# Sixteen of 32 re-laid v reads issued on ScalarE instead of SyncE, with the instruction order searched anew, in a fused attention and GEGLU block

## The chip, the cores and the metric

One core of one Trainium2 chip runs the whole program. The metric is device time in microseconds (us), the median of several executions. The kernel before takes 245.5 us; the span inside its profiled execution, first to last instruction, is 243.3 us. Executions of one kernel on one chip mostly agree within 0.3%.

## The reference, cut to what matters

```python
h = layernorm(x) * (1 + ca) + sa              # x: 2048 tokens x 512
qkv = h @ wqkv                                # 32 heads of 16
# each token looks at itself and 7 earlier tokens, 2 apart (W, dil = 8, 2)
logits = einsum('bhsd,bhswd->bhsw', q, kg) * scale ; attn = softmax(logits)
o = einsum('bhsw,bhswd->bhsd', attn, vg)
x = x + ga * (o @ wo)
h = layernorm(x) * (1 + cb) + sb
x = x + gb * ((gelu(h @ w_gate) * (h @ w_up)) @ w_down)     # 1792 wide
```

## The kernel before: the parts concerned

The tokens go through in five groups (256, 256, 512, 512, 512), called group 0 to group 4. VectorE multiplies q with shifted k (tiles `pq`) and the weights `e` with shifted v (tiles `pv`); TensorE adds the products up by matmuls. For the second product v must lie in another layout, `vR`: four blocks of 32 partitions, each shifted by two tokens more. The kernel writes v to a scratch buffer in DRAM (`scr`) and reads it back four times, about 260 KB each. That makes 8 x 4 = 32 reads, all on SyncE:

```python
for r in (0, 2, 1, 3):
    dma(P * njv * (n + 8) * 2, lambda dq, ...: dq.dma_start(
        out=t[32*r:32*r + 32, ...], in_=bass.AP(scr..., offset + 2 + 2*r, ...)),
        r=[scr], w=[(t, r)], ..., bw=185e3, late=0.7)
```

The program is a list of 1016 operations. `ORDER`, a constant list of their numbers found by a search on a planning model, fixes in which order they are emitted, and so the order on every engine.

```python
placed = [self.ops[i] for i in ORDER]
...
for o in placed:
    ...                 # take buffers, warm-up matmuls before the first real one
    o.fn()
```

The DMA semaphores are eight and go round over both queues: a transfer waits until the one eight places earlier in the list has landed.

## Time and profile before

| | before |
|---|---|
| time, median | 245.5 us |
| span of the profiled run | 243.3 us |
| first real matmul (`qkv_ps`) | 12.14 us |
| end of the last matmul | 239.41 us |
| **stream** (the difference) | **227.27 us** |
| tail after it | 3.87 us |

The last three rows are read from the timeline of PE. The span is the start plus the stream plus the tail. A stream consists of matmuls at their cadence (0.216 us for one of 512 columns in this trace) and of holes, in which TensorE stands. The prediction shows the other lines of this profile.

### The profile page before, as it was taken

Reading aid. Unit: us, or ns where it says so; the run is one execution under the profiler, and the core shown is the slowest. Engines: PE = TensorE matmul, PEld = TensorE weight load, DVE = VectorE, ACT = ScalarE, POOL = GpSimd, SP = SyncE. Lnnn points to the kernel's source line nnn. Section 1 sums busy time; section 2 is a strip of 40 time slices with the busy share of each in tenths; the row PEclk is TensorE's granted clock in tenths of the full one; section 3 lists DMA queues with packets and bytes.
Section 4 is the critical chain, followed back from the end, with each engine's and each line's share of the span. In section 5 each row is a group of like instructions: output and inputs, shape, how many; then the busy total and the mean of one; then the engine's idle time right before and its main releaser. Section 6 shows DMA issues by size and latency. Waiting matters only on the chain.

```text
span 243.3 us, 4304 instructions
## 1 busy us (share of the span) xinstructions
PE 235.3 (97%) x1660; PEld 128.2 (53%) x1680; DVE 163.4 (67%) x317; ACT 148.5 (61%) x278; POOL 25.7 (11%) x45
## 2 busy tenths in 40 slices
PE   7999999999999999999999999999999999999993
PEld 2499555644469645775443444444444444444461
DVE  3878998999999999669985577982422413221222
ACT  2288799678958763894588865328467442665400
POOL 1287212002000300120000011000000100000000
PEclk9999999999999999999999999999999999999999
DMA  5999999898999338269022904210000412000011
GB/s 162 354 316 270 195 195 211 201 238 197 270 285 274 110 94 178 60 180 142 11 65 57 221 9 90 43 43 1 3 0 0 108 26 86 0 0 0 3 43 43
DMA packets 38970, 29.10 MB, mean 120 GB/s; under 512 B 14117, under 2 KB 38054, under 8 KB 38950
## 3 DMA queue, kind: packets, MB, share of 16 engines
q1 hardware_dynamic: 38800, 28.83, 49.8%
q8 instruction: 13, 0.21, 0.4%
q14 instruction: 7, 0.06, 0.1%
q10 hardware_dynamic: 150, 0.00, 0.0%
HBM read 21.40 MB, written 4.28 MB: 106 GB/s over the span
## 4 chain that ended last, share of the span: by engine, by line
PE 70%; DVE 17%; DMA 5%; issue 2%; POOL 2%; ACT 2%; DVEq 0%; ACTq 0%; POOLq 0%
PE y_ps L827 20%; PE u_ps L800 20%; PE g_ps L800 19%; PE x_ps L777 4%; DVE pq L654 4%; DMA wqkv<-in_A_wqkv_dram 3%; DVE pq L660 3%; DVE pv L752 3%; PE o_ps L762 2%; POOL rstd L522 2%; DVE st L516 2%; PE LT L670 2%; PE qkv_ps L603 1%; DVE xn L526 1%; DMA x_sg<-in_A_x_dram 1%
## 5 line engine op out<-in xcount | busy, mean ns | idle before, releaser
L800 PE MATMUL u_ps<-h2T,Wu 128*128 128x512 bf16 (+1 forms) x280 | 54.4, 336 | 0.5 <-ACT gl L809 0.3
L800 PE MATMUL g_ps<-h2T,Wg 128*128 128x512 bf16 (+1 forms) x280 | 54.7, 337 | 0.1
L827 PE MATMUL y_ps<-WdP,hht 128*128 128x512 bf16 (+1 forms) x230 | 49.1, 366 | 0.4
L809 ACT ACTIVATE gl<-g_ps 128x512 bf16<-128x512 f32 x56 | 33.0, 603 | 25.1 <-PE g_ps L800 24.8
L603 PE MATMUL qkv_ps<-hT,wqkv 128*128 128x512 bf16 (+1 forms) x229 | 43.7, 339 | 0.1
L812 DVE TENSOR_TENSOR hht<-gl,ub 128x512 bf16<-128x512 bf16 x56 | 22.6, 422 | 28.8 <-ACT ub L811 20.3
L811 ACT CAST ub<-u_ps 128x512 bf16<-128x512 f32 x56 | 31.7, 589 | 14.9 <-PE u_ps L800 11.7
L800 PEld LDWEIGHTS <-Wg 128*128 128x128 bf16 x280 | 27.0, 98 | 23.0 <-issue 1.5
L800 PEld LDWEIGHTS <-Wu 128*128 128x128 bf16 x280 | 27.0, 98 | 22.7 <-issue 2.0
L827 PEld LDWEIGHTS <-hht 128*128 128x128 bf16 x238 | 23.1, 98 | 24.6 <-issue 0.4
L522 POOL TENSOR_TENSOR rstd<-rstd,neghalf 128x2 f32<-128x2 f32 x16 | 17.5, 1094 | 162.4 <-DVE rstd L511 140.1
L603 PEld LDWEIGHTS <-wqkv 128*128 128x128 bf16 x232 | 24.9, 114 | 13.6 <-issue 1.3
L654 DVE TENSOR_TENSOR pq<-qT,kT 128x2048 bf16<-128x2048 bf16 x24 | 28.8, 1215 | 0.3
L746 DVE TENSOR_TENSOR pv<-e,vR 128x2048 bf16<-128x2048 bf16 x24 | 28.5, 1219 | 0.0
L538 ACT ACTIVATE h2T<-h2T,modT,scl 128x512 bf16<-128x512 bf16 (+1 forms) x20 | 13.2, 726 | 15.1 <-DMA h2T<-xn 15.1
L840 DVE TENSOR_TENSOR ot<-y_ps,x_sg 128x512 bf16<-128x512 f32 (+1 forms) x13 | 8.2, 648 | 18.5 <-PE y_ps L827 18.5
L781 DVE SCALAR_TENSOR_TENSOR x_sg<-x_ps,x_sg 128x512 bf16<-128x512 f32 x16 | 11.0, 687 | 14.2 <-PE x_ps L777 7.2
L777 PE MATMUL x_ps<-woP,oT 128*128 128x512 bf16 x57 | 14.9, 379 | 0.7 <-DVE rinv L723 0.5
L508 ACT ACTIVATE xn<-x_sg,xsum 128x512 bf16<-128x512 bf16 x16 | 11.5, 721 | 4.3 <-DVE xsum L505 4.3
L516 DVE BATCH_NORM_STATS2 st<-x_sg 128x6 f32<-128x512 bf16 x16 | 10.6, 679 | 3.3 <-DMA x_sg<-in_A_x_dram 3.3
L619 ACT CAST kT<-qkv_ps 128x512 bf16<-128x512 f32 x16 | 9.5, 602 | 1.8 <-PE qkv_ps L603 1.8
L619 ACT CAST qT<-qkv_ps 128x512 bf16<-128x512 f32 x16 | 9.5, 600 | 1.3 <-PE qkv_ps L603 1.3
(93 smaller groups left out, 201.2 us busy)
## 6 DMA issues: line engine op xcount, KB each, us to landing
vR<-scr SPq DMA_DIRECT2D x24, 260.0 KB, 5.0
wm<-in_w_mod_dram SPq DMA_DIRECT2D x6, 512.0 KB, 6.7
vR<-scr SPq DMA_DIRECT2D x8, 264.0 KB, 5.2
out_dram<-ot SPq DMA_DIRECT2D x15, 128.0 KB, 1.8
Wg<-in_B_w_gate_dram SPq DMA_DIRECT2D x2, 896.0 KB, 11.0
Wu<-in_B_w_up_dram SPq DMA_DIRECT2D x2, 896.0 KB, 5.4
WdP<-in_B_w_down_dram SPq DMA_DIRECT2D x2, 896.0 KB, 12.6
scr<-vT SPq DMA_DIRECT2D x6, 264.0 KB, 2.4
```

What stands on the lines that cost most here:

```text
L516: dve(0.59, lambda i=i, st=st, c0=c0: nc.vector.bn_stats(out=st[:, i, :], in_=x[g, c0 + i]), r=[x.key(g, c0 + i)], w=[(st, i)], pri=p)
L522: gp(0.65, lambda rstd=rstd: nc.gpsimd.tensor_tensor(out=rstd[:], in0=rstd[:], in1=neghalf[:, 0:2], op=ALU.pow), r=[rstd, neghalf], w=[rst ...
L603: nc.tensor.matmul(ps[:, j - j0, :], lhsT=wqkv[b][:, dt, j:D:4], rhs=h_cols(hT, g, dt), start=(dt == 0), stop=(dt == DT - 1))
L619: act(0.475, lambda t=t, off=off, j0=j0, ps=ps: nc.scalar.copy(out=t[:, j0:j0 + nj, off:off + n], in_=ps[:]), r=[ps], w=[(t, j) for j in r ...
L654: dve(1.14, lambda j=j, wg=wg, t=pq[m]: nc.vector.tensor_tensor(out=t[:], in0=_ap(q[g][:, j, 0:n], [[0, 4], [1, n]]), in1=_ap(k[g][:, j, : ...
L746: dve(1.14, lambda jj=jj, jl=jl, wg=wg, t=pv[m]: nc.vector.tensor_tensor(out=t[:], in0=_ap(e[:, wg, :], [[0, 4], [1, n]]), in1=vR[g][jj][: ...
L777: nc.tensor.matmul(x1_ps[:], lhsT=oT[:, j, c4 * P:(c4 + 1) * P], rhs=woP[:, j, :], start=(j == 0), stop=(j == 3))
L800: nc.tensor.matmul(ps[:, ft - f0, :], lhsT=Wt[ft // 7][:, dt, ft % 7 * P:(ft % 7 + 1) * P], rhs=h_cols(h2, g, dt), start=(dt == 0), stop=( ...
L809: act(0.485, lambda gl=gl, ps=gu[0]: nc.scalar.activation(out=gl[:], in_=ps[:], func=ACT.Gelu_apprx_tanh), r=[gu[0]], w=[gl], pri=p, table ...
L811: act(0.475, lambda ub=ub, ps=gu[1]: nc.scalar.copy(out=ub[:], in_=ps[:]), r=[gu[1]], w=[ub], pri=p)
L812: dve(0.335, lambda gl=gl, ub=ub, ht=ht: nc.vector.tensor_tensor(out=ht[:], in0=gl[:], in1=ub[:], op=ALU.mult), r=[gl, ub], w=[ht], pri=p)
L827: nc.tensor.matmul(y_ps[:], lhsT=hh[ft // nf][:, ft % nf, c4 * P:(c4 + 1) * P], rhs=WdP[:, ft, c0:c0 + w], start=(ft == 0), stop=(ft == FT ...
```

## The change

The intent: half of the issues leave SyncE, on which a blocked read holds up what follows, and the order is searched again. The diff, cut:

```diff
 ORDER = [
-    55, 5, 0, 7, 8, 9, 42, 43, 40, 41, 2, 6, 13, 33, ...
+    56, 7, 0, 55, 1, 4, 8, 9, 40, 42, 41, 33, 5, 6, ...
     (all 1016 numbers anew)
...
-        lat = {... "pool": 0.45 ...}
+        lat = {... "pool": 0.15 ...}
...
-                    r=[scr], w=[(t, r)], ..., bw=185e3, late=0.7)
+                    r=[scr], w=[(t, r)], ..., bw=300e3, late=0.7,
+                    ring="act" if r > 1 else "sp")
```

`lat`, `bw`, the planner's one shared pipe and some durations (cut here) are only the planner's picture of the chip; on the chip they show through the order alone, and in one warm-up matmul more (14 for 13). One more planner's rule is cut here: the matmuls of the last output tile's two halves may only come after those of the other tiles (`after=ends`). This rule asks for a half tile at the very end.

## The prediction

> **What bounds the kernel now.** I began with the share of busy time and the chain that ended last.
>
> ```profile
> PE 235.3 (97%) x1660; PEld 128.2 (53%) x1680; DVE 163.4 (67%) x317; ACT 148.5 (61%) x278; POOL 25.7 (11%) x45
> PE 70%; DVE 17%; DMA 5%; issue 2%; POOL 2%; ACT 2%; DVEq 0%; ACTq 0%; POOLq 0%
> ```
>
> The first line says that TensorE is busy for 97% of 243.3 us, the second that 70% of the chain is matmuls and 17% VectorE. A busy PE can still be a slow one, so next I cut the span into stages (columns: stretch, its length, then the busy time of PE, weight loads, DVE, ACT and POOL with counts, granted clock, DMA share, GB/s):
>
> ```profile
> 0.00:12.00 12.00, 10.29 (x75) 4.64 (x76) 7.70 (x24) 2.39 (x6) 2.86 (x13) 1.00 0.82 257
> 12.00:66.00 54.00, 52.77 (x509) 33.94 (x513) 50.21 (x96) 45.13 (x86) 15.62 (x25) 1.00 1.03 232
> 66.00:160.00 94.00, 93.18 (x683) 52.93 (x690) 80.20 (x141) 63.06 (x117) 5.84 (x5) 1.00 0.53 123
> 160.00:220.00 60.00, 59.74 (x296) 26.73 (x300) 19.80 (x46) 32.33 (x62) 1.42 (x2) 1.00 0.09 23
> 220.00:243.30 23.30, 19.31 (x102) 9.97 (x102) 5.45 (x12) 5.53 (x11) 0.00 (x0) 1.00 0.07 23
> ```
>
> In the first 12 us PE only runs warm-up matmuls until the first third of wqkv lands; that wait stands in the chain as a DMA piece. From 12 to 220 us PE is busy for 52.77 + 93.18 + 59.74 = 205.69 of 208 us, so **all idle time there is 2.3 us**. The PE timeline shows the real matmuls starting at 12.14 us and ending at 239.42 us, and inside that stretch 16 matmuls of 128x512 take 3.46 us, 0.216 us each, with a granted clock of 1.00 throughout. PE is packed with work that has to be done. After it 3.9 us are left: one last addition on VectorE (0.69 us), the issue of the last store and its landing, and the program's end.
>
> Where the 2.3 us go, from the waits of PE:
>
> ```profile
> PE x_ps L777 <- DVE rinv L723: 0.5, 1, 0.5
> PE LT L700 <- DVE m L695: 0.4, 1, 0.4
> PE u_ps L800 <- ACT gl L809: 0.3, 1, 0.3
> ```
>
> Two are waits for VectorE, in the stage from 12 to 66 us, where VectorE is busy 93% of the time (50.21 of 54); that is also where the chain runs over VectorE. None is for a v read.
>
> Last I asked after the tile vR, the re-laid v, which this change is about, and after what the queue on SyncE waits for:
>
> ```profile
> L628 SPq DMA_DIRECT2D vR<-scr x32: 538/594/1010, 26.3 to 148.3; - x32
> L746 DVE TENSOR_TENSOR pv<-e,vR x24: 1212/1220/1225, 77.7 to 164.5; 128x2048 bf16<-128x2048 bf16 x24
> L752 DVE TENSOR_TENSOR pv<-e,vR x8: 1218/1220/1226, 38.5 to 61.1; 128x2048 bf16<-128x2048 bf16 x8
> DMA to landing us min/median/max: 3.6/5.1/10.9
> ...
> SPq L628 <- DVE pv L746: 8.1, 2, 6.3
> ```
>
> 32 reads, 0.594 us of issue each, 5.1 us to land; and the tile's list of what ended idle time before the products pv is empty: **no product of the kernel before waits for its v**. The last line says that it is the other way round in one place: SyncE's queue stood 6.3 us at one read until a product had freed the buffer, with everything behind it in that queue.
>
> **What the Trainium skill says.** "DMA: Bandwidth & Descriptors", section "Issuing engines are not separate DMA queues": transfers of all issuing engines run on the same 16 DMA engines, and using several issuers saves only the issuing sequencer's time. Not shown before, because but for four tiny loads all transfers go on SyncE; it means that I count no bandwidth as won. The same page, "Queues, rings and completion order", says that SP and ACT each own a row of rings and that an engine takes turns between the rows it has work for, packet by packet. So a read on ScalarE's ring need not wait behind megabytes queued on SyncE's. The trace before shows such queueing: the two reads issued at 49.7 and 50.3 us, behind a 0.9 MB load of Wg, took 10.6 and 10.7 us to land instead of 5.1. "Perfetto Trace Analysis", "Sequencer Loop": a sequencer reads one instruction after the other, so a transfer that must wait holds what follows on its engine; the 6.3 us above agree.
>
> **The change part by part.** I numbered the program's 1016 operations in the order in which it makes them, which the change keeps, and read both order lists by engine.
>
> 1. *SyncE loses 16 issues*: 16 x 0.594 = 9.5 us of its sequencer. It is idle for most of the span (77.2 us in waits for the norm's output alone), so nothing of it is on the path. Worth 0 directly.
> 2. *ScalarE gains 16 issues*: 16 x 0.594 = 9.5 us, on top of 148.5 us. From 12 to 66 us it is busy 45.1 of 54; I count four of the reads before its first gelu instruction's stage and some four near 66 us: up to 8 x 0.594 = 4.8 us, which makes 49.9 of 54. The new order also moves three evacuations of group 4's q and k (0.48 us of cadence each, 1.4 us) behind the first gelu, against one before. It still fits, with little slack. Later (66 to 160 us) ScalarE has 31 us free. On the path: 0 as long as no issue has to wait; PE has four one-bank buffers ahead of ScalarE, about 3.5 us of work, to ride over 0.6 us.
> 3. *Reads land earlier*, by the queueing they escape, up to some 5 us for those behind weights. Since no product waits for them now, the gain is only what the order makes of it: the new order runs group 0's four products one after the other right after their weights e, where the old put max and norm work between them, and does two pq products fewer ahead of them. Attention's chain becomes shorter; PE's work does not.
> 4. *PE's order*: same 346 operations, and I counted the switches between full and 32-column tile mode in both lists: 28 and 28. No change. ACT table loads: 7 and 7 (1.28 us each, off the path).
> 5. *The start*: SyncE's first six transfers are the same in the same order, 2.6 MB up to the first third of wqkv. The touches on ScalarE are permuted, and GpSimd makes its constants (5.4 us from 16.1 to 21.5 before) ahead of the first power; that may push this power from 5.88 to about 7 us, and the normed x was only formed at 8.39 us, so it is hidden. 0 +- 0.3.
> 6. *The tail*: before, the last PE work is a whole 512-column output tile, with 0.69 us on VectorE and a 128 KB store. After, the two half tiles are last: the addition falls to about 0.38 us (two halves took 0.76) and the store to half. Gain about 0.3 us.
> 7. The edits of latencies, rates and lanes change only the planner's picture and the count of warm-up fillers. 0.
>
> **Sum**: tail -0.3; of the 2.3 us of PE idle, perhaps a third recovered as the order is fitted better to v that arrives sooner, -0.7; misfits of a fresh order on the chip, +0.2. 245.5 - 0.8 = **244.7 us**. Even with all idle and the tail recovered it would be 245.5 - 2.3 - 0.3 = 242.9.
>
> **The rivals.**
> *A: ScalarE's queue becomes the new wait.* A read there may issue only when the relaid copy has landed, when its buffer is free, and when the transfer eight places earlier has landed (the trace's DMA semaphores go round eight, over both queues). Before, such a stand cost SyncE 6.3 us at no price; on ScalarE it would hold the evacuations, and past some 3.5 us PE would stop. For it: the new list puts one read of the last group between gelu work and the last exponential, and two of group 3 have 0.9 MB loads of w_down eight places before them. Against it: the order was made with these waits known, and those loads are long started by then. One misfit would cost 1 to 3 us: 246.5 to 248.5.
> *B: v arrives later than planned.* The planner now reckons 300 GB/s for these reads where it had 185, and group 0's products come about 2 us earlier in VectorE's list. Before, group 0's last read landed at 36.7 us with its first product at 38.55, a slack of 1.9 us. If landing does not move forward, VectorE idles 1 to 2 us in the stage where it leads: 246 to 247.
> *C: nothing happens.* The transfers were hidden and stay so, and PE's packed stream sets the time: 245.2 to 245.5. Everything in the waits speaks for it.
> *D: a large gain* needs a shorter start or fewer matmuls; the change has neither.
>
> **Range and chances.** C and the modest gain are the bulk, 243.3 to 245.6; A and B together I give a quarter, mostly below 248. So 243.2 to 247.2 holds it 8 times in 10. Faster by over 2% means under 240.6, below the floor of 242.9: 0.01. Slower by over 2% means over 250.4, several misfits together: 0.03.
>
> **What would show it.** Right: PE busy unchanged within 1 us, still starting near 12.1 us and idle for 1 to 2.5 us between 12 and 220; 16 issues on each queue; the last VectorE addition 128x256 instead of 128x512; no wait of pv for vR; ScalarE's idle time before evacuations still put down to PE. Wrong: waits of PE for ScalarE of over 1 us each just after a vR issue (A), waits of pv for vR around 37 us (B), or a first real matmul that moved by over 0.5 us (step 5).

## The result, and the profile after

243.37 us (243.31 to 243.78, four runs) against 245.47 (245.25 to 245.95, four runs). The ratio is 0.9915 with an interval of 0.9897 to 0.9934.

The stages of the changed kernel (columns as in the prediction):

```profile
0.00:12.00 12.00, 9.27 (x76) 4.52 (x78) 7.39 (x23) 2.31 (x6) 6.79 (x28) 1.00 0.82 265
12.00:66.00 54.00, 53.72 (x538) 35.52 (x541) 52.17 (x98) 46.65 (x90) 11.29 (x10) 1.00 1.00 252
66.00:160.00 94.00, 93.09 (x665) 51.97 (x672) 79.78 (x141) 61.27 (x113) 3.84 (x5) 1.00 0.48 110
160.00:220.00 60.00, 59.84 (x299) 26.90 (x302) 19.94 (x47) 34.79 (x64) 1.38 (x2) 1.00 0.10 25
220.00:241.70 21.70, 18.17 (x98) 9.38 (x96) 4.77 (x10) 4.43 (x8) 0.00 (x0) 1.00 0.08 25
```

From 12 to 220 us PE is busy for 53.72 + 93.09 + 59.84 = 206.65 of 208, so idle for 1.35 us where it was 2.3. (Some 0.6 to 0.8 us of either figure is an artefact: 12 to 16 matmul records are missing from these two traces, and PE seems idle for 0.05 us beside each. The stream, from its first record to its last, doesn't suffer from that: 227.27 and 225.66 us.) In the second row VectorE does 52.2 us of work where it did 50.2: in the stage where it is nearly full, it stands 2 us less. What it waited for in that stage (12 to 66 us), first before, then after:

```profile
DVE xn L526 <- POOL rstd L522: 2.7, 5, 0.7
DVE pq L660 <- ACT qT L619: 0.5, 1, 0.5
```

```profile
DVE e L737 <- PE rB L733: 0.9, 1, 0.9
DVE xn L527 <- POOL rstd L523: 0.2, 1, 0.2
DVE x_sg L783 <- PE x_ps L779: 0.2, 1, 0.2
```

Before, it stood five times for GpSimd's power, 2.7 us in all; after, once for 0.2 us. What PE waits for from 12 to 220 us in the changed kernel, where the prediction showed three lines of before:

```profile
PE u_ps L802 <- ACT gl L811: 0.4, 1, 0.4
PE y_ps L829 <- issue: 0.2, 1, 0.2
```

Both waits for VectorE are gone. And the reads, by queue:

```profile
L629 ACTq DMA_DIRECT2D vR<-scr x16: 546/547/1498, 22.9 to 148.0; - x16
L629 SPq DMA_DIRECT2D vR<-scr x16: 538/562/1337, 27.5 to 134.6; - x16
...
its engine sat idle before it (us, times) until:
  issue: 1.1, 1
  DMA vR<-scr: 1.1, 1
```

Sixteen on each, as intended. But now VectorE stands twice before a product of v, 1.1 us each, which it never did before: at 73.5 us, where the profile names no releaser ("issue"), and at 152.7 us, where it is a read issued on ScalarE at 148.0. The ring that was to bring v sooner goes together with v that comes too late somewhere. That made me ask which half of the change had won.

The last addition, before and after (start, duration, tile):

```profile
239.45 0.69 DVE L840 TENSOR_TENSOR ot<-y_ps,x_sg 128x512 bf16<-128x512 f32 x1 [0.76 <-PE y_ps L827]
```

```profile
238.26 0.42 DVE L843 TENSOR_TENSOR ot<-y_ps,x_sg 128x256 bf16<-128x256 f32 x1 [0.51 <-PE y_ps L829]
```

### The profile page after: what moved, and what is told of

Its sections match the earlier page's. It is cut to its first block, busy times and chain, and to the rows that moved or that the text cites. A ratio compares the mean times of both kernels' runs of the same rounds, so it can differ in the third digit from the quotient of the medians.

```text
span 241.7 us, 4320 instructions
## 1 busy us (share of the span) xinstructions
PE 234.1 (97%) x1664; PEld 128.3 (53%) x1681; DVE 164.1 (68%) x317; ACT 149.5 (62%) x278; POOL 23.3 (10%) x45
## 4 chain that ended last, share of the span: by engine, by line
PE 84%; DVE 6%; DMA 5%; issue 1%; ACT 1%; SPq 0%; POOL 0%; ACTq 0%
PE y_ps L829 20%; PE u_ps L802 18%; PE qkv_ps L604 17%; PE g_ps L802 16%; PE x_ps L779 5%; PE o_ps L764 3%; PE LT L672 3%; DMA vR<-scr 3%; DMA x_sg<-in_A_x_dram 2%; DVE pv L748 2%; DVE WdP L866 1%; DVE st L517 1%; PE LT L702 1%; PE rB L733 1%; DVE hht L814 1%
## 5 line engine op out<-in xcount | busy, mean ns | idle before, releaser
L814 DVE TENSOR_TENSOR hht<-gl,ub 128x512 bf16<-128x512 bf16 x56 | 23.1, 422 | 36.1 <-ACT ub L813 26.3
L813 ACT CAST ub<-u_ps 128x512 bf16<-128x512 f32 x56 | 32.1, 589 | 13.6 <-PE u_ps L802 13.1
L770 ACT CAST oT<-o_ps 128x512 bf16<-128x512 f32 x16 | 9.2, 600 | 8.1 <-PE o_ps L764 8.1
```

The costliest lines, as they stand in the source:

```text
L813: act(0.475, lambda ub=ub, ps=gu[1]: nc.scalar.copy(out=ub[:], in_=ps[:]), r=[gu[1]], w=[ub], pri=p)
L814: dve(0.335, lambda gl=gl, ub=ub, ht=ht: nc.vector.tensor_tensor(out=ht[:], in0=gl[:], in1=ub[:], op=ALU.mult), r=[gl, ub], w=[ht], pri=p)
```

## The experiments

Theory 1: the order alone made the gain. Theory 2: the ring made it, or made the order possible. Two more questions: is a hole of TensorE worth its length, and what does a DMA issue on ScalarE cost?

The table puts all traces together (the time is the median of all runs; start, stream and tail are read from the timeline of PE in the one profiled run). Chip calls are four, the first two on one chip and the last two on another; the kernel before was run beside each, at 245.19, 245.62, 245.09 and 245.25 us.

| kernel (call) | time | ratio to before | start | stream | tail |
|---|---|---|---|---|---|
| before | 245.47 | 1 | 12.14 | 227.27 | 3.87 |
| changed | 243.37 | 0.9915 | 12.56 | 225.66 | 3.43 |
| new_order_all_sync (1) | 242.91 | 0.9905 | 12.74 | 225.12 | 3.43 |
| old_order_split (1) | 260.66 | 1.0578 | 11.94 | 244.95 | 3.88 |
| old_order_new_tail (1) | 244.61 | 0.9965 | 11.69 | 227.29 | 3.45 |
| new_order_early_scale (1) | 244.03 | 0.9945 | 12.20 | 226.72 | 3.47 |
| old_order_filled (2) | 246.22 | 1.0004 | 12.97 | 227.77 | 3.91 |
| new_order_all_scalar (2) | 254.16 | 1.0353 | 12.45 | 235.60 | 3.44 |
| new_order_again (3) | 243.77 | 0.9943 | 13.08 | 226.06 | 3.44 |
| new_order_sync_again (3) | 242.70 | 0.9908 | 12.22 | 225.09 | 3.43 |
| new_order_group2_sync (3) | 242.63 | 0.9898 | 12.37 | 225.12 | 3.46 |
| old_order_split_timed (3) | 250.14 | 1.0179 | 11.87 | 233.46 | 3.86 |
| old_order_filled_again (4) | 245.17 | 0.9982 | 12.50 | 227.67 | 3.87 |
| new_order_sync_shift (4) | 242.90 | 0.9906 | 12.42 | 225.13 | 3.47 |

**1. The new order without the ring.**

```diff
-                    ... late=0.7, ring="act" if r > 1 else "sp")
+                    ... late=0.7)
```

> The new order unchanged, but all 32 reads of v issued on SyncE again, each at its place in the order. Theory 1 (the order alone made the gain; the ring is free but useless, as no product waits for v in a way that reaches TensorE): 243.2 to 243.8 us, as the changed kernel. Theory 2 (the ring made the new order possible: on one queue the reads stand behind weights, transposes and waits, products come late and TensorE runs dry in the stage from 12 to 80 us): at least 1 us lost, 244.5 us or more, with waits of the products pv for vR of over 1 us in sum more than in the changed kernel.

242.91 us, under the range of theory 1 even. Theory 2 falls: with all reads back on SyncE, nothing of the gain goes. Run again (experiment 5), this kernel left a trace in which TensorE waits for nothing from its first real matmul to its last (stretch, length, busy time of PE with its count, then the other columns):

```profile
12.22:237.31 225.09, 225.09 (x1601) 123.41 (x1599) 155.78 (x289) 146.77 (x273) 12.64 (x17) 1.00 0.48 114
```

So 225.09 us is what this order's matmuls take. The changed kernel's stream stands 0.57 us above it and the old one's 2.18 (about 0.2 of that is four transposes, which the new order runs before the first real matmul).

**2. The old order with the ring.**

```diff
-                    ... bw=185e3, late=0.7)
+                    ... bw=185e3, late=0.7, ring="act" if r > 1 else "sp")
```

> The old order unchanged, with the 16 reads of shifts 2 and 3 issued on ScalarE at their old places. Theory 1 (order alone): no gain, 245.2 to 245.8 us if ScalarE never has to stand at a read; the reads were hidden before. Theory 2 (ring): a gain of some 0.5 us or more by the ring itself. Rival A of the prediction (a read that must wait holds ScalarE's queue): slower, 246 to 249 us, because in the old order the reads stand where SyncE could wait at no price (it stood 6.3 us at one), with waits of TensorE for ScalarE of over 1 us.

260.66 us, 15 us slower than before. Its profile is of clock 0.98, but its four fast runs took 257.6 to 261.0 us as well, three of them at that clock and the fastest at 0.993. So part of the 15 us is slower matmuls and not waiting: in the stream PE is busy for 231.5 of 244.95 us here and for 226.5 us in experiment 3, at a clock of 1.00. Why the clock is lower here isn't shown. The other 13.5 us PE stands (2.3 before). The tile vR and the waits of PE in it:

```profile
its engine sat idle before it (us, times) until:
  DMA vR<-scr: 19.1, 6
```

```profile
PE o_ps L763 <- DVE pv L747: 5.0, 4, 2.5
PE o_ps L763 <- DVE pv L753: 4.9, 3, 4.0
```

None of the theories had the right picture. ScalarE's evacuations are not held by its reads, and TensorE waits for ScalarE only 0.3 us, as before. It is the reads that are held: ScalarE reaches a read only after all that the list has before it. VectorE then waits 19.1 us for v, and TensorE for VectorE. Compare the issue times of a few of the reads (each read's own number in the list; from the two traces):

```
read             SyncE, before   ScalarE, old order split
74  (group 0)    31.70 us        34.49 us
167 (group 1)    47.36 us        59.87 us
317 (group 2)    64.10 us        83.70 us
744 (group 4)   131.09 us       162.06 us
```

Some of the later difference is delay piled up, but read 167 is 12.5 us late where the kernel had lost only a few. In the old list it stands behind a ScalarE copy that ran at 58.5 us. On SyncE, which only issues transfers, it ran ahead of that place and went out at 47.4 us. **A late place in the list costs nothing on an idle engine's queue, and its full lateness on a busy engine's.**

**3. The same split, with the reads moved forward in the list**, each to just before the ScalarE instruction that ran when SyncE used to issue it (16 numbers moved by 9 to 79 places; no other edit).

> The old order, split over both rings, but each of the 16 reads on ScalarE moved forward in the order (by 9 to 79 places) to just before the ScalarE instruction that ran when SyncE used to issue that read. Theory (the split ran 15 us slow because ScalarE reaches a read only when it has run all that the list has ahead of it, which is 2 to 32 us after SyncE issued it): nearly all of the loss goes, 245 to 247 us, the rest being 16 issues of 0.55 us. Rival (reads on ScalarE are harmful wherever they stand, by holding the evacuations): over 250 us, with TensorE's waits now for ScalarE.

250.14 us, ratio 1.0179 (1.0139 to 1.0219): of the 15 us about 10 come back, 5 remain. Part of the 10 is the clock (1.00 in this profile, 0.98 in the last). By TensorE's idle time in the stream, 13.5 us went down to 7.0, where the old order has 2.3. The place of the read is thus the larger part of the loss. The theory's range is missed; the rival's "over 250" is just met, but not its picture. What remains, from the waits of PE:

```profile
PE u_ps L803 <- DMA Wu<-in_B_w_up_dram: 2.6, 1, 2.6
PE qkv_ps L605 <- ACT vT L621: 2.5, 2, 2.0
```

Reordering the transfers also reorders who waits for whom among the eight semaphores and pushes the load of Wu back; that explains the first line at least in kind, but I didn't separate the two. In the second line TensorE does wait for ScalarE, but no read held it there: ScalarE stood 2.15 us, until 36.5 us, for a transposed load of hT, and the copy of vT came behind that.

**4. All 32 reads on ScalarE, new order.**

```diff
-                    ring="act" if r > 1 else "sp")
+                    ring="act")
```

> The new order with all 32 reads on ScalarE instead of 16, so twice the issue time there (another 16 x 0.55 = 9 us). Theory (ScalarE has slack and buffers ahead of TensorE, its issues are off the path): within 0.5 us of the changed kernel, 243.2 to 243.9 us. Rival A (issues or their waits on ScalarE hold the evacuations): over 1 us slower than the changed kernel, with waits of TensorE for ScalarE between 40 and 135 us of over 0.5 us each, just after a read.

254.16 us, over 10 us slower. Here the rival's picture does appear, twice. ScalarE's timeline around the first place, and PE's:

```profile
41.12 0.17 ACT L467 ACTIVATE scl<-modT_ps 128x4 f32<-128x4 f32 x1
43.39 0.55 ACTq L629 DMA_DIRECT2D vR<-scr  x1
43.98 0.58 ACT L770 CAST oT<-o_ps 128x512 bf16<-128x512 f32 x1 [2.69 <-DMA Wg<-in_B_w_gate_dram]
```

```profile
44.62 1.69 PE L779 MATMUL x_ps<-woP,oT 128*128 128x512 bf16 x6 [1.94 <-ACT oT L770]
```

The read waits for a semaphore whose last holder is a load of Wg, 0.9 MB. The wait itself is no bar in the timeline: the read starts when it may go, at 43.39 us, and the time before is only a gap. The Trainium skill says so ("Perfetto Trace Analysis", "DMA Instruction — HWDGE (DVE, Sync)": the reported start is when all semaphores are satisfied), and this trace agrees. The copy of `oT` behind it is 2.7 us late, TensorE stands 1.94 us. The second place is at 72.25 us: a read waits for a load of WdP, ScalarE stands 3.8 us and TensorE 0.98 us, at 74.8. But the largest hole of this trace comes from late v again. VectorE waits 5.4 us for a read, the product `hht` stands behind, and TensorE waits for that:

```profile
93.25 1.23 DVE L748 TENSOR_TENSOR pv<-e,vR 128x2048 bf16<-128x2048 bf16 x1 [5.41 <-DMA vR<-scr]
94.39 0.42 DVE L814 TENSOR_TENSOR hht<-gl,ub 128x512 bf16<-128x512 bf16 x1
```

```profile
94.87 2.74 PE L829 MATMUL y_ps<-WdP,hht 128*128 128x512 bf16 x7 [4.12 <-DVE hht L814]
```

So of TensorE's named holes 4.1 us are late reads and 2.9 a held ScalarE; how the whole 10 us split I have not measured, as the clock was lower too (0.987 to 0.993 in all six runs).

**5. Does the ring cost something in the changed kernel?** I ran it again beside the kernel of experiment 1, and beside one with only group 2's four ScalarE reads moved back to SyncE.

```diff
-                    ring="act" if r > 1 else "sp")
+                    ring="act" if r > 1 and g != 2 else "sp")
```

> The changed kernel once more, unaltered, as the yardstick of this call on its chip: 0.85% under the kernel before (interval 0.66 to 1.03%), so about 243.3 us where that kernel takes 245.4.

> The new order with all reads on SyncE once more, beside the changed kernel on one chip. Its trace lacks a 0.55 us hole of TensorE at 76.3 us, which the changed kernel has (u_ps waits for ScalarE's gelu). If the ring costs that hole: 0.3 to 0.6 us faster than the changed kernel. If the difference of the two medians so far (0.46 us) was chip and start: within 0.15 us.

> The changed kernel with the four ScalarE reads of group 2 (issued at 60.2 and 65.2 to 67.5 us, three in a row, 2.2 us of ScalarE) moved to SyncE, the other 12 left on ScalarE. Theory: these issues made the gelu late that TensorE waits for at 76.3 us; the hole of 0.55 us goes, and the time is that of the kernel with all reads on SyncE within 0.2 us. Rival (the hole comes from elsewhere, or the other 12 cost as well): the hole stays, time as the changed kernel.

243.77, 242.70 and 242.63 us. The ring costs 0.5 to 1 us (1.1 us by these medians; the streams differ by 0.97 us, and by 0.54 between the changed kernel's first trace and experiment 1), and group 2's reads are all of it: their move alone gives the time, and the stream (225.12 us), of the kernel with all reads on SyncE. The intervals of the ratios (0.991 to 0.9977 with the ring, 0.9872 to 0.9924 with group 2's reads moved) just overlap, so the times alone wouldn't settle it; the traces do. The chain can be followed from engine to engine in the changed kernel. ScalarE, 65 to 69 us:

```profile
65.17 0.58 ACT L813 CAST ub<-u_ps 128x512 bf16<-128x512 f32 x1
65.17 0.55 ACTq L629 DMA_DIRECT2D vR<-scr  x1
65.76 0.59 ACT L620 CAST kT<-qkv_ps 128x512 bf16<-128x512 f32 x1
65.86 1.65 ACTq L629 DMA_DIRECT2D vR<-scr  x2
67.54 1.28 ACT L811 ACT_TABLE_LOAD   x1 [1.19 <-issue]
```

Three reads in a row, at the place that the list gives them. The first is issued while the copy runs and costs ScalarE nothing; the other two leave it idle for 1.19 us. But it is the first that comes too late. In the list it is number 317, the last of the four blocks that VectorE's first product of group 2 reads; the other two (322 and 324) belong to the group's second tile, which is used from 83.9 us on. With group 2's reads on SyncE the four went out from 57.5 to 61.2 us, number 317 at 58.2. The product, here in the changed kernel and then with those reads on SyncE:

```profile
73.53 2.36 DVE L748 TENSOR_TENSOR pv<-e,vR 128x2048 bf16<-128x2048 bf16 x2 [1.12 <-issue]
75.81 0.75 DVE L814 TENSOR_TENSOR hht<-gl,ub 128x512 bf16<-128x512 bf16 x2
```

```profile
72.24 2.36 DVE L748 TENSOR_TENSOR pv<-e,vR 128x2048 bf16<-128x2048 bf16 x2
74.52 0.75 DVE L814 TENSOR_TENSOR hht<-gl,ub 128x512 bf16<-128x512 bf16 x2
```

The profile names no releaser for the 1.12 us, and it lacks the landing of read 317. That the product waits for it is inferred: `e`, its other input, was ready at 72.4 us, read 322, issued 0.7 us after 317, landed at 75.5, and the wait goes when 317 is issued earlier. The product `hht` behind it is 1.3 us late (0.2 of it is this run's later start), the gelu that waits for it (its buffer) is late with it, and TensorE stands:

```profile
76.97 1.91 PE L802 MATMUL u_ps<-h2T,Wu 128*128 128x256 bf16 x16 [0.38 <-ACT gl L811]
```

That hole is missing in all four traces with group 2's reads on SyncE, and it is in the other two with half of all reads on ScalarE in the new order (0.79 us in new_order_again, 0.39 in new_order_early_scale). VectorE's second wait for v, at 152 us, is in all of these traces, with 0.6 to 1.3 us, on either queue; TensorE doesn't wait behind it.

**6. The tail alone**: the old order, with only its last 30 operations in the new relative order.

```diff
-    ... 1006, 1007, 1013, 1008, 1014, 1015, 1000, 1001, 1009, 1002, 1003,
+    ... 1006, 1007, 1010, 1011, 1012, 1008, 1002, 1013, 1014, 1009, 1003, 1015,
```

> The old order with only the last 30 operations (the last group's output tiles) in the order that the change gives them, so that a half tile comes last. Prediction step 6: the tail after the last matmul shrinks by 0.3 to 0.4 us and TensorE's 0.2 us hole just before the end goes: 244.9 to 245.2 us. If the end is set by the store's landing and not by VectorE's last addition: no change within 0.1 us.

244.61 us, ratio 0.9965 (0.9931 to 0.9998). The tail is 3.45 us for 3.87, and the stream is the old one to 0.02 us. The step is right: 0.42 us.

**7. An earlier start**: two VectorE operations of the first group put ahead of the statistics of a later tile (numbers 53 and 54 before 275 in the list).

> The changed kernel with two of VectorE's operations (the scale and shift of the first group's hT) put ahead of the statistics of a later tile, since in its trace the first real matmul starts 0.42 us later than before and waits for these. Theory: every us that TensorE starts earlier, or does not stand, is a us of the end, as its stream is packed to the end: start at 12.2 to 12.3 us and no hole of 0.24 us just after, together 0.4 to 0.6 us faster than the changed kernel, 242.8 to 243.0 us. Rival (the stage from 12 to 66 us is bound by VectorE's chain, so an earlier start is used up in a later wait): 243.2 to 243.5 us, with the TensorE idle time coming back between 20 and 70 us.

244.03 us, no gain over the changed kernel (ratios to before 0.9945 and 0.9915, with intervals that overlap) and over the rival's range. The rival's picture is the right one: TensorE started earlier, at 12.20 us, and gave it back at 22 us, where it waits for the delayed product:

```profile
22.92 0.40 PE L674 MATMUL LT<-pq,Mph 128*32 128x256 bf16 x8 [0.61 <-DVE pq L664]
```

**8. Filling the old order's two holes** at 49 and 65 us, each with a qkv tile that was ready (500 before 121 and 719 before 346).

> The old order, all reads on SyncE, with two of TensorE's operations swapped: one qkv tile moved ahead of the projection that stood 0.62 us for the reciprocal at 48.9 us, and one ahead of the maximum's subtraction that stood 0.61 us at 65.2 us. Theory (the stream of matmuls sets the end; a hole filled with work that is ready is a gain of its whole length): 1.0 to 1.2 us faster than before, 244.2 to 244.5 us. Rival (VectorE's chain sets the stage from 12 to 66 us; what is moved ahead delays the chain and the hole comes back behind it): 245.2 to 245.7 us, with new holes of the same sum.

> The old order with its two holes of TensorE at 49 and 65 us filled, once more, as the first run of it fell on lower granted clocks (0.99) and was no answer. Theory (a hole filled is a gain of its length): 1.0 to 1.2 us faster than before. Rival (VectorE's chain sets this stage and the hole comes back behind): within 0.3 us of before, with holes of the same sum a few us later.

In the first run the profile and two more of the six runs fell on granted clocks of about 0.99 (ratio 1.0004, 0.9966 to 1.0042); the second gives 0.9982 (0.9944 to 1.002), no gain. The two holes are gone, and PE's timeline shows what came in their place some us later (pieces of it, in order of time):

```profile
56.08 0.61 PE L672 MATMUL LT<-pq,Mph 128*32 128x512 bf16 x8 [0.21 <-DVE pq L656]
70.59 0.83 PE L672 MATMUL LT<-pq,Mph 128*32 128x512 bf16 x12 [0.21 <-DVE pq L656]
72.07 1.92 PE L802 MATMUL u_ps<-h2T,Wu 128*128 128x256 bf16 x16 [0.65 <-DMA Wu<-in_B_w_up_dram]
```

So these two holes of TensorE were symptoms; VectorE's chain, and once the landing of Wu, set the stage from 12 to 72 us in the old order. Swapping neighbours on TensorE did not help.

One more variant was built, with a reciprocal on VectorE moved ahead of its neighbour (185 before 336). It never ran: VectorE would read a PSUM bank that TensorE may still be writing.

**9. One small step more on the best kernel**: all reads on SyncE, and operation 54 ahead of three tiny ones.

> The new order with all reads on SyncE, and one operation of VectorE (the second scale and shift of the first group's hT) put ahead of three tiny ones (0.17 us each), for the hole of 0.24 us just after TensorE's start. If that hole is worth its length: 0.1 to 0.3 us faster than the kernel with all reads on SyncE, about 242.5 us where the kernel before takes 245.1, the fastest of all. If the stage from 12 to 22 us is bound by VectorE, as the kernel with both of these moved far ahead showed with its hole of 0.78 us at 22 us: no gain, 242.7 to 242.9 us.

242.90 us beside 245.25; no gain over 242.70 beside 245.09. The hole after the start is gone (it is not in new_order_sync_again either, without this edit) and one of 0.19 us at 21.9 us has come.

The fastest kernels are thus the new order with all reads on SyncE, or with the reads split except group 2's: about 242.7 us, 0.9% to 1% under before, against 0.6% to 0.85% for the changed kernel.

## Why the prediction was right or wrong

The forecast, 244.7 us with a range of 243.2 to 247.2, holds the measured 243.37 near its lower edge. The class (within 2%) and the direction are right; the gain, 0.8 us, is too small by half or more (2.1 us by the medians, 1.6 by the two profiled runs). That the range held is in part luck: its largest term, -0.7, rested on v that arrives sooner, and v did not (step 3 below). By its own steps:

- **The bound** is right: a packed stream of matmuls sets the end. PE stays near 235 us busy, 234.1 after (1.0 of the difference lies before 12 us, in the warm-up); the floor of 242.9 that was worked out from the idle time is close to the 242.6 to 242.9 us of the best variants. One reading was loose: the three waits shown under "where the 2.3 us go" make 1.2 us, and some of the rest is records missing from the trace.
- **Step 6, the tail**, is right: -0.3 predicted, -0.44 in the trace, -0.42 where it was done alone.
- **The term of the sum that was mis-sized** is "of the 2.3 us of PE idle, perhaps a third recovered ... -0.7; misfits ... +0.2". The stream shrank by 1.61 us with the ring and by 2.15 us without. I took a third because I read the holes as fixed by VectorE; I saw from the page that VectorE is 93% busy there, but didn't ask what its own idle 3.8 us wait for. 2.7 of them were GpSimd's power, a wait of which the new order left 0.2 us. That this wait and the shorter stream go together is measured; that it is the cause among 1016 moved operations is inferred, as no run moved it alone.
- **Step 3, reads land earlier because of their own ring**, failed, and it was the reason given for the -0.7. ScalarE's reads in the changed kernel still took up to 9.6 us to land while two 0.9 MB loads were in flight on SyncE, against 10.3 us for a SyncE read issued behind the same loads. Experiment 1 shows the gain without the ring. The sign "no wait of pv for vR" failed too.
- **Step 2, ScalarE's cost**: counted as 16 x 0.594 us beside the path. A single issue hides behind the instruction that runs. But "on the path: 0" was wrong by 0.5 to 1 us, through group 2's reads (experiment 5): not by blocked evacuations, but by late v.
- **Rival A** named the right engine with the wrong arrow. A read can hold ScalarE's queue (seen with 32 reads there), but in the split order it is ScalarE's queue that holds the reads. **Rival B**, v later than planned, did happen, but at 73 us, for 1.1 us, instead of at 37 us, and for another reason: the place of the read in ScalarE's queue. **Rival C** is wrong in that the order did gain.
- **Step 5, the start**: 0 +- 0.3 predicted, 0.42 us later in the profiled run. Over the traces it scatters from 11.7 to 13.1 us, with the same program too (12.56 and 13.08 for the changed kernel), so no shift is shown.
- **Steps 4 and 7** are as counted: 28 tile-mode switches in either trace (mostly 0.31 us from the start of one matmul to that of the next, for 0.216 without a switch) and seven table loads.

## What to carry to other kernels

In these runs a DMA issued from a busy engine went out when that engine's program reached it, not when its data were ready (read 167: 59.9 us for 47.4). Before moving issues off an idle queue, compare when that queue issued them with when the busy one will get there. When a change has two parts, run each alone: here one part made all the gain, the other cost 0.5 to 1 us with the new order and 15 us with the old. And before filling a hole on the leading engine, ask what the engine behind it waits for; a hole that is a symptom comes back.

## What the Trainium skill lacked or had wrong

- "DMA: Bandwidth & Descriptors", "Issuing engines are not separate DMA queues": it says what a second issuing engine saves, and these runs agree that no bandwidth is won (from 12 to 66 us the new order moved 249 to 252 GB/s with both rings in use and 245 to 249 with SyncE's). That section lacks the price, that the issue stands in program order behind that engine's compute: up to 12.5 us late for an early read and 260.7 us for 245.2 in the whole (old_order_split, of which some 5 us are a lower clock).
- The same page, "Queues, rings and completion order": taking turns between rows at packet level made me expect that a read on the other row escapes queued bulk loads. Here it landed after 9.6 us beside 10.3 us for one in the same row. I drew the conclusion, the page doesn't state it; a number there would have helped.
- "Perfetto Trace Analysis", "Sequencer Loop": an engine instruction is pushed on while the sequencer goes on, so a single issue on ScalarE is hidden behind a running copy (both start at 65.17 us), but of three in a row 1.19 us showed as idle. The pages give what an issue costs a sequencer only roughly, and give no measured figure for a compute engine; here it is 0.55 us of ScalarE's.
